# Second mixture of a three-stage kernel: sums of weights between the row tiles, late weight splits moved, 28 filling transposes for 40

## The chip, the cores and the metric

The kernel runs on one core of one Trainium2 chip. The metric is the device time of one execution in microseconds (us). Three runs of the kernel before took 1088.09, 1088.69 and 1091.23 us; their median, 1088.69, is the time before.

## The reference

Three stages follow one another. An attention without softmax makes x from q, k and v; a first mixture of 8 experts sends each of 4608 tokens to its best expert; a second mixture spreads the result over 8 experts of exactly 576 tokens each. The change lies in the second mixture alone:

```python
N, D, E, F = (4608, 512, 8, 1024)
logits = x @ w_gate
# tokens are assigned in order of their logits, at most N // E per expert
for e in range(E):
    mask = assigned == e
    h = np.maximum(x[mask] @ w1[e], 0.0)
    out[mask] = h @ w2[e]
```

## The kernel before

**Precision.** Each f32 operand of a matrix product is held as two parts: a high part, cast on ScalarE (names whi, xqh, and the first half of hx), and a low part, the difference, made on VectorE (wlo, xql, second half of hx). A product is three matmuls: high by high, high by low, low by high.

**The order of the work** is the order in which the program issues it; each of the five engines has its own queue and takes its instructions in that order, waiting where an operand or a buffer is not ready. TensorE (PE) multiplies and transposes, VectorE (DVE) and ScalarE (ACT) prepare operands and empty the accumulators, GpSimd (POOL) issues the gathers of token rows and the scatters of results, and SyncE (SP) issues the loads of weights.

**Expert 0 of the second mixture** is computed plainly. `rows_in(0)` gathers its rows from ybuf (L2064), `warm2` lets TensorE do transposes of a constant while they come (NWARM, L38: 40 of them, L1623). `xplain` (L1649) transposes a tile of 128 rows (tp, two buffers in turn) and splits it (L1654, L1655). `plain1` (L1662) is one of eight product groups of the first layer, 256 weight columns by one half of the tokens, with the relu and its low part (L1659, L1660). The weights are split by `wcast` (L555): the cast on ScalarE (L567), the low part on VectorE (L573), which can be put off into the list CAST; three raw buffers (wraw) rotate, so a load waits for the low part three weights earlier.

**Experts 1 to 7** do the first layer in `seven` (L1907): seven products in place of eight, of sums and differences of weight and input blocks. For these, `first_units` and `rest_units` (generators, one `yield` per step) form the next expert's weights during the work of the one before: sums ws on VectorE (L1793), high parts on ScalarE (L1800), low parts on VectorE (L1797). `xraw` (L1686) transposes a row tile of the next expert and copies it to xb on ScalarE (L1694, L1696); `xsums` forms the sums of inputs (L1708, L1711, L1714).

**The second layer**, `layer2_r` (L2023), has four full row tiles t and a small fifth one. Each full tile is eight groups kf of three matmuls (L2039 to L2041), and after each group `between(t, kf)` issues a piece of the next expert's preparation: a row tile at five places (XAT, L1683) and one step of a generator. The last, small tile is L2035, sixteen matmuls into mD. In the kernel before, the remaining steps of `first_units` run in one go ahead of the second layer (L2112):

```python
run_gen(ga)
gb = rest_units(e + 1)
```

Of the kernel before, what the change touches and what calls it, by code (L numbers as in the profile page):

```python
# [34 lines left out]

PW = (0, 0.8, 2.9, 2.1, 2.0)

NWARM = (18, 40, 6)  # L38

ASIDE = (1, 5, 5, 5, 3)  # L40

# [35 lines left out]
def fused_kernel(ctx, tc, q, k, v, g_norm, emb, tau, w1, w2, wgate, v1, v2, out):  # L77
    nc = tc.nc
    V = nc.vector
# [29 lines left out]
    def mk(pool, shape, dtype, name, **kw):  # L109
        if pool is mp:  # L110
            pool = MP[name in MP0]
        return pool.tile(shape, dtype, name=name, **kw)
# [6 lines left out]
    def src(t, off, ap):  # L119
        return bass.AP(tensor=t.tensor, offset=t.offset + off, ap=ap)  # L120
# [101 lines left out]
    def run_gen(g):  # L222
        for _ in g:
            pass
# [318 lines left out]
    WS = {"load": 0, "cast": 0}  # L543
# [3 lines left out]
    def wload(upto, q=nc.sync):  # L547
        while WS["load"] < min(upto, len(WQ)):
            key, t, off, pat = WQ[WS["load"]]
            raw = mk(wpA, [128, 1024], F32, "wraw", bufs=3)  # L550
            q.dma_start(raw.rearrange("p (a c) -> p a c", c=pat[-1][1]), src(t, off, pat))
            RAW[key] = raw
            WS["load"] += 1

    def wcast(n=1, eng=None, ahead=3, later=None, load=True):  # L555
        for _ in range(n):
            if WS["cast"] >= len(WQ):
                return
            wload(WS["cast"] + 1)
            key = WQ[WS["cast"]][0]  # L560
            raw = RAW.pop(key)

            i = WS["cast"] // (RING // 2)
            wp = WP[(i + (i > 2 * E - 2)) % 2]
            hi = mk(wp, [128, 1024], F32R, "whi")
            lo = mk(wp, [128, 1024], F32R, "wlo")
            nc.scalar.copy(hi, raw)  # L567
            WT[key] = (hi, lo)
            WS["cast"] += 1
            up = WS["cast"] + ahead  # L570

            def rest(eng, lo=lo, raw=raw, hi=hi, up=up):
                eng.tensor_tensor(lo, raw, hi.bitcast(F32), op=OP.subtract)  # L573
                if load:
                    wload(up)
            if later is None:
                rest(eng or V)
            else:
                later.append(rest)
# [292 lines left out]
    def warm(n):  # L872
        pw = mk(psum, [128, 512], F32, "sm")
        for i in range(n):
            nc.tensor.transpose(pw[:, 128 * (i % 4):128 * (i % 4) + 128], ident, ident)
# [45 lines left out]
    for n, st in enumerate(steps):  # L921
        gi, u, hg = st
        i = n % len(UNITS)
# [528 lines left out]
    SIDE, LATER, CAST = [], [], []  # L1452
# [134 lines left out]
    CAST.pop(0)(V)  # L1587
    warm(NWARM[0])
    with tc.If(nc.values_load(fli[0:1, 1:2], min_val=0, max_val=1) > 0, label="gen"):  # L1589
# [30 lines left out]
    def warm2(n):  # L1620
        pw = bank(0)
        for i in range(n):
            nc.tensor.transpose(pw[:, 0, 128 * (i % 4):128 * (i % 4) + 128], ident, ident)  # L1623
# [6 lines left out]
    def turned(e, t, n):  # L1630

        xg = XG.pop((1, e, t))
        pt = mk(ps2, [128, KD, 128], F32, "tp", bufs=2)
        for kd in range(KD):
            nc.tensor.transpose(pt[:, kd, :n], xg[:n, kd * 128:(kd + 1) * 128], ident[:n, :n])  # L1635
        if e == 0 and e not in XQ:
            XQ[e] = [mk(mp, [128, 7, 2, T2], F32R, f"xq{p}") for p in "hl"]
        return xg, pt

    def token(e, t, n, xg):  # L1640

        ti = mk(mp, [128, 1], I32, "ti", bufs=12)
        V.tensor_copy(ti[:n], xg[:n, HD:HD + 1].bitcast(I32))
        TI[e, t] = ti

    def plain_x(e):
        return [x.rearrange("p q k c -> p (q k c)")[:, :KD * C2].rearrange("p (k c) -> p k c", k=KD) for x in XQ[e]]

    def xplain(e, i):  # L1649

        c, t, n = TL[1, e][i]
        xg, pt = turned(e, t, n)
        hi, lo = (x[:, :, 128 * t:128 * t + n] for x in plain_x(e))
        nc.scalar.copy(hi, pt[:, :, :n])  # L1654
        V.tensor_tensor(lo, pt[:, :, :n], hi.bitcast(F32), op=OP.subtract)  # L1655
        token(e, t, n, xg)
# [116 lines left out]
    def sraw(*key):  # L1773
        return SR[SI[key]]

    def sdone(*key):
        over.add(SI[key])
        sload()
# [4 lines left out]
    def unit():  # L1783
        i = UN[0] % 6
        UN[0] += 1
        return [mk(wpB, [128, 1024], F32R, nm) if i < 4 else mk(mp, [128, 1024], F32R, nm, bufs=2) for nm in ("whi", "wlo")]

    def put(e, u, *ng):
        for i, k in enumerate(ng):
            SW[(e, *k)] = [x[:, 512 * i:512 * i + 512].rearrange("p (a c) -> p a c", a=2) for x in u]  # L1790

    def tt(o, a, b, op):
        V.tensor_tensor(o, a, b, op=op)  # L1793

    def lo(u, x, i=None):
        h, l = (u if i is None else [w[:, 512 * i:512 * i + 512] for w in u])
        V.tensor_tensor(l, x, h.bitcast(F32), op=OP.subtract)  # L1797

    def hi(u, x, i=None):
        nc.scalar.copy(u[0] if i is None else u[0][:, 512 * i:512 * i + 512], x)  # L1800
# [26 lines left out]
    def rest_units(e):  # L1827

        sa, sb, a22 = AH[e]
        u2 = unit()  # L1830
        put(e, u2, ("S3", 0), ("S2", 0))
        hi(u2, sa)
        yield
        u3 = unit()
        put(e, u3, ("S1", 0), ("S4", 0))
        hi(u3, sb)
        lo(u2, sa)
        yield
        u4 = unit()
        put(e, u4, ("A22", 0), ("A11", 1))  # L1840
        hi(u4, a22, 0)
        lo(u3, sb)
        yield
        r0, r1 = sraw(e, 0, 1, 0), None
        hi(u4, r0[:, :512], 1)
        lo(u4, a22, 0)
        sdone(e, 0, 0, 1)
        yield
        u5 = unit()
        put(e, u5, ("A12", 1), ("S3", 1))  # L1850
        hi(u5, r0[:, 512:], 0)
        lo(u4, r0[:, :512], 1)
        yield
        r1 = sraw(e, 0, 1, 1)
        a11, a12, a21, a22 = r0[:, :512], r0[:, 512:], r1[:, :512], r1[:, 512:]
        sa, sb = (mk(mp, [128, 1024], F32, "ws", bufs=2) for _ in range(2))
        s2, s1, s3, s4 = sa[:, :512], sa[:, 512:], sb[:, :512], sb[:, 512:]
        tt(s1, a21, a22, OP.add)
        yield
        tt(s2, s1, a11, OP.subtract)  # L1860
        yield
        u6 = unit()
        put(e, u6, ("S2", 1), ("S1", 1))
        hi(u6, sa)
        tt(s3, a11, a21, OP.subtract)
        yield
        hi(u5, s3, 1)
        lo(u5, a12, 0)
        yield
        lo(u6, sa)  # L1870
        yield
        tt(s4, a12, s2, OP.subtract)
        sdone(e, 0, 1, 0)
        yield
        lo(u5, s3, 1)
        AH[e] = s4, a22
        yield
# [191 lines left out]
    rows_in(0)  # L2069
    warm2(NWARM[1])  # L2070
    xplain(0, 0)
    warm2(NWARM[2])
    xplain(0, 1)
    warm2(NWARM[2])
    wload(WS["cast"] + 1, nc.scalar)
    while CAST:
        CAST.pop(0)(V)
    wload(WS["cast"] + 3)
    wcast()
    def step(g, n=1):  # L2080
        for _ in range(n):
            next(g, None)

    def chain(*gs):
        for g in gs:
            yield from g()

    ga = chain(lambda: first_units(1))
    for i, (f, c) in enumerate(((0, 0), (1, 0), (0, 1), (1, 1), (2, 0), (2, 1), (3, 0), (3, 1))):
        plain1(0, f, c, (i + 1) % 3)  # L2090
        if i == 0:
            xplain(0, 2)
            xplain(0, 3)
        if i == 1:
            xplain(0, 4)
        if i < 4:
            wcast()
            if i == 3:
                sload()
        else:  # L2100
            step(ga, 2 if i in (4, 6) else 1)
        if i == 3:
            nc.gpsimd.drain()
            rows_in(1)
    for e in range(E):
        more = e + 1 < E
        if e > 0:
            ga = chain(lambda: first_units(e + 1)) if more else iter(())
            seven(e, ga)
        pairs(e)  # L2110
        if more:
            run_gen(ga)  # L2112
            gb = rest_units(e + 1)
            XS = []

            def between(t, kf):
                if (t, kf) in XAT:
                    xraw(e + 1, XAT[t, kf])
                elif (t, kf) == (1, 5):
                    XS.append(xsums(e + 1))  # L2120
                if XS and kf % 2:
                    step(XS[0])
                else:
                    step(gb)
            layer2_r(e, (0, 1), 0, between)
            layer2_r(e, (2, 3), 1, between)
            run_gen(gb)
            run_gen(XS[0])
            layer2_r(e, (4,), 2)
        else:  # L2130
            for i, tt_ in enumerate(((0, 1), (4,), (2,), (3,))):
                layer2_r(e, tt_, (0, 2, 1, 0)[i])
# [24 lines left out]
```

## Time and profile before

| | |
|---|---|
| median of the runs | 1088.69 us |
| the profiled execution | 1088.42 us, span 1086.6 us |
| TensorE busy | 1026.8 us (94%) |
| VectorE busy | 727.5 us (67%) |
| ScalarE busy | 523.7 us (48%) |
| GpSimd busy | 291.8 us (27%) |
| mean granted TensorE clock | 0.974 of full speed |
| share of the DMA queue of SP | 34.4% |

The span runs from the first to the last instruction of the profiled execution; its own time is 1.8 us longer. Busy is the time in which an engine has an instruction in work. All times in rows are counted from the span's start. The second mixture begins at about 641 us. A wait is idle time of an engine just ahead of an instruction, put down to the instruction that released it.

### The profile page before, as it was taken

How to read it: one execution, taken by the hardware profiler on the slowest of the kernel's cores; microseconds unless marked ns; L12 is line 12 of the kernel's file. 1: busy time of each engine (PE TensorE's matmuls, PEld its weight loads, DVE VectorE, ACT ScalarE, POOL GpSimd, SP SyncE). 2: the span in 40 equal slices, each digit the busy share in tenths (PEclk: the TensorE clock that was granted, in tenths of full speed). 3: DMA queues.
4: the chain of work that ended last, by engine and by line, in shares of the span. 5: the costliest groups of instructions: out<-in, count | busy, mean ns of one | idle time of the engine just before them, and what ended most of it. 6: DMA issues, size and time to landing. Idle time of an engine off the chain costs nothing. (4 is left out here: it accounts for less than half of the span.)

```text
span 1086.6 us, 20563 instructions
## 1 busy us (share of the span) xinstructions
PE 1026.8 (94%) x8237; PEld 942.4 (87%) x8237; DVE 727.5 (67%) x1434; ACT 523.7 (48%) x911; POOL 291.8 (27%) x389
## 2 busy tenths in 40 slices
PE   7888699999999999999999999999999999999998
PEld 7777598999999999999889879897979797979796
DVE  4467965487878696976567656666767676666760
ACT  2567635644536354435441314555555555555551
POOL 2011446516143241616001112221213131212111
PEclk8999799999999999999999999999999999999999
DMA  9999665452524443433311035242424242424211
GB/s 287 380 349 311 211 180 180 143 156 77 186 86 153 121 138 118 134 122 98 117 40 59 26 108 181 87 157 95 149 89 154 87 156 88 157 84 159 80 62 44
DMA packets 94615, 152.35 MB, mean 140 GB/s; under 512 B 11286, under 2 KB 52246, under 8 KB 94514
## 3 DMA queue, kind: packets, MB, share of 16 engines
q1 hardware_dynamic: 84994, 121.65, 34.4%
q0 software_dynamic: 8992, 28.80, 8.3%
q8 instruction: 66, 1.08, 0.4%
q10 hardware_dynamic: 528, 0.52, 0.2%
q14 instruction: 35, 0.29, 0.1%
HBM read 121.14 MB, written 29.82 MB: 139 GB/s over the span
## 5 line engine op out<-in xcount | busy, mean ns | idle before, releaser
L691 PE MATMUL mm<-xh,whi 128*128 128x256 f32 (+8 forms) x512 | 156.0, 305 | 3.4 <-DVE hl L709 3.2
L736 PE MATMUL mm<-hh,whi 128*128 128x256 f32 (+8 forms) x512 | 156.9, 306 | 0.2 <-ACT hh L708 0.2
L692 PE MATMUL mm<-xl,whi 128*128 128x256 f32 (+8 forms) x512 | 153.3, 299 | 0.3 <-DVE xl L662 0.3
L737 PE MATMUL mm<-hl,whi 128*128 128x256 f32 (+8 forms) x512 | 152.4, 298 | 1.1 <-DVE hl L1504 0.6
L693 PE MATMUL mm<-xh,wlo 128*128 128x256 f32 (+8 forms) x512 | 153.2, 299 | 0.0
L738 PE MATMUL mm<-hh,wlo 128*128 128x256 f32 (+8 forms) x512 | 152.1, 297 | 0.0
L833 DVE SCALAR_TENSOR_TENSOR rc<-xg,big 128x512 bf16<-128x512 f32 x128 | 110.9, 867 | 2.6
L573 DVE TENSOR_TENSOR wlo<-wraw,whi 128x1024 fp32r<-128x1024 f32 x72 | 90.7, 1262 | 21.8 <-ACT whi L567 21.3
L691 PEld LDWEIGHTS mm<-xh,whi 128*128 128x128 f32 x512 | 98.3, 192 | 5.0 <-DVE hl L709 3.6
L736 PEld LDWEIGHTS mm<-hh,whi 128*128 128x128 f32 x512 | 97.4, 190 | 2.2 <-ACT hh L708 0.5
L737 PEld LDWEIGHTS mm<-hl,whi 128*128 128x128 f32 x512 | 97.6, 191 | 1.5 <-DVE hl L1504 0.8
L692 PEld LDWEIGHTS mm<-xl,whi 128*128 128x128 f32 x512 | 98.2, 192 | 0.5 <-DVE xl L662 0.5
L693 PEld LDWEIGHTS mm<-xh,wlo 128*128 128x128 f32 x512 | 98.3, 192 | 0.0
L738 PEld LDWEIGHTS mm<-hh,wlo 128*128 128x128 f32 x512 | 97.4, 190 | 0.0
L745 ACT COPY yT<-mm 128x512 f32<-128x512 f32 (+8 forms) x31 | 19.9, 642 | 156.2 <-PE mm L738 156.2
L2054 POOL DMA_INDIRECT out<-tm,ti x40 | 42.5, 1062 | 185.1 <-ACT tm L2052 165.5
L640 POOL DMA_INDIRECT xg<-xbuf,tabi x40 | 43.1, 1077 | 171.5 <-ACT sj L599 77.4
L567 ACT CAST whi<-wraw 128x1024 fp32r<-128x1024 f32 x72 | 75.1, 1046 | 3.7 <-DMA wraw<-in_moe_w 3.7
L708 ACT ACTIVATE hh<-mm 128x512 fp32r<-128x512 f32 (+7 forms) x56 | 36.8, 657 | 73.2 <-PE mm L693 73.2
L1797 DVE TENSOR_TENSOR wlo<-wraw,whi 128x1024 fp32r<-128x1024 f32 (+1 forms) x63 | 60.6, 980 | 11.6 <-ACT whi L1800 11.6
L634 POOL TENSOR_TENSOR xg<-xg,gB 128x512 f32<-128x512 f32 (+7 forms) x37 | 61.7, 1668 | 2.9
L2064 POOL DMA_INDIRECT xg<-ybuf,tab x40 | 44.1, 1103 | 59.1 <-SPq L1589 25.5
(357 smaller groups left out, 2682.4 us busy)
## 6 DMA issues: line engine op xcount, KB each, us to landing
wraw<-in_moe_w SPq DMA_DIRECT2D x127, 512.0 KB, 3.5
kmain<-in_k SPq DMA_DIRECT2D x16, 576.0 KB, 9.0
vmain<-in_v SPq DMA_DIRECT2D x16, 576.0 KB, 10.7
xbuf<-xo SPq DMA_DIRECT2D x16, 528.0 KB, 12.5
ybuf<-yr SPq DMA_DIRECT2D x32, 260.0 KB, 2.2
qmain<-in_q SPq DMA_DIRECT2D x16, 512.0 KB, 9.8
xg<-in_moe_w SPq DMA_DIRECT2D x16, 256.0 KB, 3.9
xg<-in_moe_w_gate SPq DMA_DIRECT2D x8, 256.0 KB, 4.4
```

Source lines behind the costliest of these rows:

```text
L567: nc.scalar.copy(hi, raw)
L573: eng.tensor_tensor(lo, raw, hi.bitcast(F32), op=OP.subtract)
L634: eng.tensor_tensor(x, x, gB[:n, None, :].to_broadcast([n, H, D]), op=OP.mult)
L691: nc.tensor.matmul(o, a, xh[:, kd, :N], start=(kd == 0), stop=False)
L692: nc.tensor.matmul(o, a, xl[:, kd, :N], start=False, stop=False)
L693: nc.tensor.matmul(o, b, xh[:, kd, :N], start=False, stop=(kd == KD - 1))
L736: nc.tensor.matmul(o, a, hh[:, kf, :N], start=(kf == 0), stop=False)
L737: nc.tensor.matmul(o, a, hl[:, kf, :N], start=False, stop=False)
L738: nc.tensor.matmul(o, b, hh[:, kf, :N], start=False, stop=(kf == KF - 1))
L833: V.scalar_tensor_tensor(junk, raws[i], 1.0, wgB[:, x], op0=OP.mult, op1=OP.mult, accum_out=w2g[:, i // KF, i % KF, x:x + 1])
L1797: V.tensor_tensor(l, x, h.bitcast(F32), op=OP.subtract)
L2064: nc.gpsimd.indirect_dma_start(out=xg[:n, :YP], out_offset=None, in_=ybuf[:, :], in_offset=bass.IndirectOffsetOnAxis(ap=tab2[:n, e * SC + ...
```

## The change

Three edits, all in the second mixture:

1. *Filling transposes.* 28 in place of 40 ahead of expert 0's first rows.
2. *Expert 0's late weight splits.* Of the low parts left in CAST, one goes where all went; the next follows the fifth row tile, after the second product group. The five `wcast` that ran ahead of the loop and in its groups 0 to 3 run in groups 1 to 5. Expert 1's raw loads (`sload`) begin in group 5 in place of 3, its `first_units` take one step in group 6 and two in group 7, in place of six steps in groups 4 to 7.
3. *Sums of weights.* The steps of `first_units` that are left after the first layer are no longer run in one go. They are chained ahead of those of `rest_units`, so `between` issues one after each matmul group. Where the chain is used up, the step goes to `xsums`, in even groups too.

```diff
-NWARM = (18, 40, 6)
+NWARM = (18, 28, 6)
...
-    while CAST:
-        CAST.pop(0)(V)
-    wload(WS["cast"] + 3)
-    wcast()
+    CAST.pop(0)(V)
...
         if i == 0:
             xplain(0, 2)
             xplain(0, 3)
+            wload(WS["cast"] + 2)
         if i == 1:
             xplain(0, 4)
-        if i < 4:
+            CAST.pop(0)(V)
+            wload(WS["cast"] + 3)
+        if 0 < i < 6:
             wcast()
-            if i == 3:
+            if i == 5:
                 sload()
-        else:
-            step(ga, 2 if i in (4, 6) else 1)
+        if i > 5:
+            step(ga, i - 5)
...
         if more:
-            run_gen(ga)
-            gb = rest_units(e + 1)
+            gb = chain(lambda: ga, lambda: rest_units(e + 1))
...
-                if XS and kf % 2:
-                    step(XS[0])
-                else:
-                    step(gb)
+                if XS and kf % 2 or next(gb, 0) == 0:
+                    for x in XS:
+                        step(x)
```

ScalarE's queue before, from expert 1's last relu (L1938) into its second layer; whi<-ws is the high part of a unit of sums for expert 2, xb<-tp the copy of a transposed row tile:

```order
L1938 ACTIVATE hx<-tm 128x2x288
L1800 CAST whi<-ws 128x1024
L1694 COPY xb<-tp 128x4x128
L1800 CAST whi<-ws 128x1024
L1800 CAST whi<-wraw 128x512
L1694 COPY xb<-tp 128x4x128
L1800 CAST whi<-wraw 128x512 x2
L1696 COPY xb<-tp 128x8x32
```

The same place of ScalarE's queue in the changed kernel:

```order
L1938 ACTIVATE hx<-tm 128x2x288
L1694 COPY xb<-tp 128x4x128 x2
L1800 CAST whi<-ws 128x1024
L1696 COPY xb<-tp 128x8x32
L1800 CAST whi<-ws 128x1024
L1800 CAST whi<-wraw 128x512 x3
L1694 COPY xb<-tp 128x4x128 x2
```

The copies of row tiles 0 and 1 have moved ahead of the first unit of sums, the small third one ahead of the second unit.

VectorE's queue before, at expert 0's first two product groups; hx<-mB and hx<-mD are the low parts of the hidden layer of groups 0 and 1, xql the low part of a row tile, wlo that of a weight:

```order
L573 TENSOR_TENSOR wlo<-wraw,whi 128x1024 x3
L1660 SCALAR_TENSOR_TENSOR hx<-mB,hx 128x2x256
L1655 TENSOR_TENSOR xql<-tp,xqh 128x4x128
L1643 COPY ti<-xg 128x1
L1655 TENSOR_TENSOR xql<-tp,xqh 128x4x128
L1643 COPY ti<-xg 128x1
L573 TENSOR_TENSOR wlo<-wraw,whi 128x1024
L1660 SCALAR_TENSOR_TENSOR hx<-mD,hx 128x2x256
L1655 TENSOR_TENSOR xql<-tp,xqh 128x4x64
L1643 COPY ti<-xg 64x1
L573 TENSOR_TENSOR wlo<-wraw,whi 128x1024
```

The same place of VectorE's queue in the changed kernel:

```order
L573 TENSOR_TENSOR wlo<-wraw,whi 128x1024
L1660 SCALAR_TENSOR_TENSOR hx<-mB,hx 128x2x256
L1655 TENSOR_TENSOR xql<-tp,xqh 128x4x128
L1643 COPY ti<-xg 128x1
L1655 TENSOR_TENSOR xql<-tp,xqh 128x4x128
L1643 COPY ti<-xg 128x1
L1660 SCALAR_TENSOR_TENSOR hx<-mD,hx 128x2x256
L1655 TENSOR_TENSOR xql<-tp,xqh 128x4x64
L1643 COPY ti<-xg 64x1
L573 TENSOR_TENSOR wlo<-wraw,whi 128x1024 x2
```

Of three splits ahead of the first hidden part one is left, the split ahead of the second one is gone, and two follow the fifth row tile.

## Rows read from the trace of the kernel before

**Rows 1.** The page, part 1: busy us, share of the span, instructions.

```profile
PE 1026.8 (94%) x8237; PEld 942.4 (87%) x8237; DVE 727.5 (67%) x1434; ACT 523.7 (48%) x911; POOL 291.8 (27%) x389
```

**Rows 2.** Waits of TensorE, 700 to 1086 us: total us, times, longest.

```profile
PE tp L1635 <- ACT xb L1694: 14.9, 6, 2.5
```

**Rows 3.** Timeline of TensorE, expert 1: start, duration, instruction, idle before and releaser.

```profile
730.49 0.60 PE L1635 MATMUL tp<-ident,xg 128*128 128x128 f32 x4
...
736.78 0.46 PE L1635 MATMUL tp<-ident,xg 64*128 64x64 f32 x4 [2.47 <-ACT xb L1694]
...
741.86 0.60 PE L1635 MATMUL tp<-ident,xg 128*128 128x128 f32 x4
```

**Rows 4.** Timeline of VectorE, the same place.

```profile
732.86 1.69 DVE L1793 TENSOR_TENSOR ws<-wraw 128x512 f32<-128x512 f32 x2
734.48 0.68 DVE L1793 TENSOR_TENSOR ws<-ws,wraw 128x512 f32<-128x512 f32 x1
```

**Rows 5.** Timeline of ScalarE, the same place.

```profile
730.76 0.69 ACT L1938 ACTIVATE hx<-tm 128x576 fp32r<-128x576 f32 x1 [1.48 <-DVE tm L1932]
735.19 1.04 ACT L1800 CAST whi<-ws 128x1024 fp32r<-128x1024 f32 x1 [3.75 <-DVE ws L1793]
736.14 0.58 ACT L1694 COPY xb<-tp 128x512 f32<-128x512 f32 x1
```

**Rows 6.** Stretches of 2 us: busy time by engine, granted clock, DMA share, GB/s.

```profile
736.00:738.00 2.00, 1.22 (x8) 1.03 (x9) 1.52 (x2) 2.00 (x4) 0.00 (x0) 1.00 0.41 129
...
790.00:792.00 2.00, 2.00 (x9) 1.55 (x9) 1.79 (x4) 2.00 (x4) 0.00 (x0) 0.63 0.82 262
792.00:794.00 2.00, 2.00 (x6) 1.56 (x5) 1.97 (x7) 1.07 (x3) 0.00 (x0) 0.51 0.16 16
```

**Rows 7.** The chain that ended last: the last row tiles of three experts.

```profile
703.32 3.67 PE mD L2035 x16
...
756.41 3.67 PE mD L2035 x16
...
1029.74 3.67 PE mD L2035 x16
```

**Rows 8.** VectorE: timeline at the end of expert 1's layer; waits, 729 to 757 us.

```profile
750.34 2.75 DVE L1711 TENSOR_TENSOR xql<-xb,xqh 128x576 fp32r<-128x576 f32 x4
760.72 0.68 DVE L2050 TENSOR_TENSOR tm<-mD,tm 64x512 f32<-64x512 f32 x1 [7.63 <-ACT tm L2049]
...
DVE wlo L1797 <- ACT whi L1800: 0.5, 2, 0.3
```

**Rows 9.** Timeline of VectorE in expert 0's second layer.

```profile
681.03 1.04 DVE L1793 TENSOR_TENSOR ws<-wraw,ws 128x512 f32<-128x512 f32 x1
...
696.17 2.76 DVE L1711 TENSOR_TENSOR xql<-xb,xqh 128x576 fp32r<-128x576 f32 x4
```

**Rows 10.** Expert 0's product groups: a wait of TensorE; timelines of VectorE and ScalarE.

```profile
PE mA L1672 <- DVE ti L1643: 1.1, 1, 1.1
...
657.80 0.68 DVE L1660 SCALAR_TENSOR_TENSOR hx<-mD,hx 128x512 fp32r<-128x512 f32 x1
658.40 0.41 DVE L1655 TENSOR_TENSOR xql<-tp,xqh 128x256 fp32r<-128x256 f32 x1
...
656.48 0.60 ACT L1659 ACTIVATE hx<-mD 128x512 fp32r<-128x512 f32 x1 [0.49 <-PE mD L1673]
```

**Rows 11.** The fill: timelines of TensorE and GpSimd; landings after issue.

```profile
643.59 3.44 PE L1623 MATMUL mA<-ident 128*128 128x128 f32 x30 [0.92 <-issue]
...
647.95 0.60 PE L1635 MATMUL tp<-ident,xg 128*128 128x128 f32 x4
...
643.41 0.95 POOL L2064 DMA_INDIRECT xg<-ybuf,tab  x1 [0.30 <-issue]
...
xg<-ybuf,tab POOLq DMA_INDIRECT x1, 4.3
...
DMA to landing us min/median/max: 3.2/4.1/6.2
```

## The prediction

> **What bounds the kernel now.** The busy shares come first: TensorE 94% of a span of 1086.6 us, the other engines 67% and less [rows 1]. So the end is set by TensorE, and a change helps only where TensorE stands idle or runs at half clock. The second view is the list of its waits in the seven later experts of the second mixture. There is one kind only: six times, 14.9 us in total, 2.5 us at the longest, the transposes of gathered rows wait for ScalarE's copy xb [rows 2]. The timeline of expert 1 shows one of them: the third tile's transposes start at 736.78 after 2.47 us of idle time [rows 3]. They write a transpose tile (two rotate) whose first user, row tile 0, has not been copied out yet.
>
> Why not is read from the two engines behind it. ScalarE is free at 731.45, but next in its queue stands the high part of a unit made of sums (L1800, whi<-ws). It waits 3.75 us, to 735.19, and the copy of row tile 0 queues behind it and starts at 736.14, although its transposes had ended at 731.09 [rows 3, 5]. That high part waits for the three sums which VectorE makes in one go after the expert's last split, the last one ending at about 735.16 [rows 4].
>
> Each stall costs more than its length. After the one of expert 2 the granted clock is 0.63 and 0.51 in the next two stretches of 2 us, the lower of the two levels, 1.2 GHz; after expert 1's it stays at 1.00 [rows 6]. The chain gives the price: from one expert's last row tile to the next is 53.09 us for expert 1 (703.32 to 756.41), but 54.67 on average for the next five ((1029.74 - 756.41)/5) [rows 7]. The first period holds a stall without a clock drop, so a drop costs 54.67 - 53.09 = 1.58 us.
>
> **The change part by part.** *Sums made one by one.* The four sums (s1, s3, s2, s4) leave the burst and take the first four steps between matmul groups; nothing is added on TensorE. What matters is ScalarE's order: the copies of row tiles 0 and 1 now stand ahead of the first unit of sums. The first can run from 731.45, where ScalarE is free, the second as soon as its own transposes end, so the third tile's transposes find their tile empty at 736.78 - 2.47 = 734.31. The stall goes, six times: **-14.9 us** (bounds 0, if another wait takes its place, and 14.9). With the gaps gone I also take away the five drops: **-7.9 us** (5 x 1.58; bounds 0 and 7.9).
>
> What is late next? VectorE's sums are no earlier than before: s2 still ends near 735.2, the unit's high part runs 735.19 to 736.23 as now, then the copy of the third tile, no longer than the 0.58 us of a full one [rows 5], to about 736.8. The next user of that transpose tile is the fifth set of transposes, at 741.86 now and 739.4 without the stall [rows 3]: 2.6 us of margin. The fourth set uses the other tile, whose copy came second. Further on, the sums of inputs end at 753.1 (750.34 + 2.75) and VectorE then idles 7.63 us [rows 8]; the next products start at 756.41 + 3.67 = 760.08 now and at 757.6 then, so 4.5 us of cover is left for the instructions that were moved. The sums of inputs get more steps late in the layer (once the units are done, odd and even steps serve them), so none is left over for the end. SP's queue of weight loads waits for the same releases by VectorE (s4, the low parts) in the same order, at about the same times.
>
> *Expert 0.* Only three of its six first steps are now done before its second layer, so the low part, s1, s3 and s2 stand ahead of s4, which ended at 682.07. That puts VectorE about 3 us later at the layer's end: 698.93 + 3 = 702, against products at 703.32 + 3.67 = 706.99 [rows 7, 9]. That hides it; without cover it would cost up to 3 us once. Since three loads on SP's queue (two plain tiles and the first raw block for expert 1) wait for low parts made one to two steps later, they go out later too. A cast that waits for one would keep a relu behind it on ScalarE; the second layer reads those values in its third row tile, so I cost this at nothing, within the same 3 us.
>
> *Late weight splits.* On VectorE two splits leave the place ahead of expert 0's first hidden part, and they and later ones go behind the fifth row tile. The hidden layer's second low part now starts at 657.80, behind a split, though its relu on ScalarE is done at 656.48 + 0.60 = 657.08; the fifth tile's low part follows it to 658.81. TensorE waits 1.1 us for that [rows 10]. Without the split both come 0.7 us earlier: **-0.7 us** (bounds 0 and 1.1, the whole wait). The moved splits are due only at the fifth and seventh product group, several us later.
>
> *28 filling transposes.* Thirty take 3.44 us, so twelve take 1.4 us [rows 11]. Whatever that does for the first gathered rows, the second ones, issued at 643.41, landed 4.3 us later, at 647.7, and their transposes start at 647.95 now [rows 11]; 1.4 us earlier would be 646.6. TensorE stands idle for about 1.1 us ahead of them instead, and the gain is **-0.2 us**. Bounds: -1.4, if the rows land earlier, and +1.6, if this gap costs one clock drop at the price above. I take the value nearest to the row that decides, the landing.
>
> The Trainium skill (DMA: Bandwidth & Descriptors, "Anatomy of one DMA — SWDGE (gpsimd) path") gives such a transfer about 2 us plus its bytes at 436 GB/s, for 128 rows of 520 floats an estimate of 2.6 us. By that page the second rows would be there at 646.0 and all of the 1.4 us would be gained, 1063.8 in the end; the 4.3 us of the row speak against it, and the measurement decides.
>
> The sum: 14.9 + 7.9 + 0.7 + 0.2 = 23.7 us off the profiled execution's own 1088.42, 1064.7. The median of the runs shown lies 0.27 above that execution, so **1065.0**.
>
> **The rivals.** *The clock falls all the same.* If the drops come from something other than the gap, only the waits go: 1088.7 - 15.8 = 1072.9. For it: expert 1's gap is as long and cost no clock. Against: the one shown begins right behind its gap [rows 6], and the other four stand at the same place of their periods.
>
> *A new wait at the transposes.* The third tile's copy now stands behind the unit of sums on ScalarE. If ScalarE falls behind there by 1.3 us more than the 2.6 us of margin in each of the six layers, half of the stall returns, too short to cost clock: 1065.0 + 6 x 1.25 = 1072.5. For it: that copy still waits for s2. Against: the margin itself.
>
> *The gathered rows land sooner* in most executions and the shorter fill pays in full: 1063.8. For it: the landings of the gathers there vary between 3.2 and 6.2 us [rows 11]; against: the median of 4.1, which is near the row I used.
>
> *Slower.* The one mechanism large enough is the handover to the next expert: the sums of weights and inputs are spread over more steps, so VectorE and ScalarE might wait for one another at each, and the products of the next expert would wait. It decides from 4.5 us of lengthening on, and to eat 23.7 us in seven handovers it needs 4.5 + 3.4 = 7.9 us in each. Ten us would give 1065.0 + 7 x 5.5 = 1103.5. Against: the instructions are the same ones in another order, and between 736 and 753 VectorE waits for 0.5 us in all now [rows 8].
>
> *The change doesn't do what it says:* if ScalarE's copies still came behind the unit, nothing would move and about 1087.8 would be left. The order of ScalarE's queue speaks plainly against it.
>
> **How the numbers follow.** The forecast 0.78, by itself 1062.5 to 1068; rows landing sooner 0.05; clock falls all the same 0.06; new wait 0.08; slower 0.02; nothing moves 0.01. The range 1062 to 1070 holds the first two, and leaves out 0.17. A difference of 0.3% (3.3 us) is about what a measurement can tell from no change. Faster by more: 0.78 + 0.05 + 0.06 + 0.08 = 0.97; within it 0.01; slower 0.02.
>
> **What would show it.** In the profile after: no wait of the transposes for xb left in TensorE's list; granted clock 1.00 from expert 1 to the end of the layers; 50.6 us (53.09 - 2.47) from one last row tile to the next; on ScalarE two xb copies ahead of the first whi<-ws, which still waits for the sums; expert 0's wait for the low part down from 1.1 to about 0.4 us; a wait of about 1.1 us for the second rows behind the fill. I am wrong if the period stays above 52 us, whatever the wait is then called, or if TensorE waits for weights or inputs at the start of an expert's products.

## The result, and the profile after

| | before | after |
|---|---|---|
| median of the runs | 1088.39 us (1087.05 to 1091.23, 4 runs) | 1063.40 us (1062.60 to 1064.35, 4 runs) |
| span of the profiled execution | 1086.6 us | 1061.9 us |
| mean granted TensorE clock | 0.974 | 0.985 |

The ratio is 0.9767, with a 95% interval of 0.9746 to 0.9789: 25 us faster, where 1065.0 had been forecast from a median that was then 1088.69. The first view is the page's line of busy times, which answers to [rows 1]:

```profile
PE 1015.7 (96%) x8225; PEld 933.9 (88%) x8225; DVE 725.1 (68%) x1434; ACT 525.4 (49%) x911; POOL 294.6 (28%) x389
```

Twelve instructions less on TensorE, the filling transposes; on every other engine the counts are the same. So the change did not save work; it saved waiting and, as the stretches below show, time at the lower clock. Where, is told by the chain of work, which answers to [rows 7]: the last row tiles of experts 0, 1 and 6.

```profile
701.82 3.67 PE mD L2035 x16
752.38 3.67 PE mD L2035 x16
...
1005.02 3.66 PE mD L2035 x16
```

The six periods between the first and the last of these take 303.20 us; before they took 1029.74 - 703.32 = 326.42. That is 23.22 of the 24.7 us between the two spans. The rest can be placed too. From the first filling transpose to expert 0's last row tile it is 61.07 us (640.75 to 701.82) against 61.93 (641.39 to 703.32), 0.86 less. The fill itself began 0.64 sooner, through stages ahead of it that were not changed: chance. From 1005.02 to the end it is 56.9 us, as before (1086.6 - 1029.74).

The list of TensorE's waits from 640 us to the end (total, times, longest), which answers to [rows 2, 10], has six entries of one wait each, and none of them lies behind 660 us. The five longest:

```profile
PE mA L1623 <- issue: 0.9, 1, 0.9
PE tp L1635 <- DMA xg<-ybuf,tab: 0.7, 1, 0.7
PE mA L1671 <- ACT xqh L1654: 0.6, 1, 0.6
PE mA L1623 <- PEq L1589: 0.4, 1, 0.4
PE mA L1672 <- DVE xql L1655: 0.4, 1, 0.4
```

ScalarE's timeline at the place of [rows 5] shows why:

```profile
729.27 0.69 ACT L1938 ACTIVATE hx<-tm 128x576 fp32r<-128x576 f32 x1 [1.48 <-DVE tm L1932]
729.86 0.57 ACT L1694 COPY xb<-tp 128x512 f32<-128x512 f32 x1
731.46 0.59 ACT L1694 COPY xb<-tp 128x512 f32<-128x512 f32 x1 [1.03 <-PE tp L1635]
733.71 1.05 ACT L1800 CAST whi<-ws 128x1024 fp32r<-128x1024 f32 x1 [1.66 <-DVE ws L1793]
734.66 0.36 ACT L1696 COPY xb<-tp 128x256 f32<-128x256 f32 x1
```

The first copy runs right behind the last relu, the second as soon as its own transposes end. The unit of sums still waits for VectorE, but the one copy behind it, the third, ends at 735.02, ahead of the transposes that use its tile next (737.83, below). TensorE's third and fifth sets of transposes, against [rows 3]:

```profile
732.75 0.46 PE L1635 MATMUL tp<-ident,xg 64*128 64x64 f32 x4
...
737.83 0.60 PE L1635 MATMUL tp<-ident,xg 128*128 128x128 f32 x4
```

No wait stands at either. And the two stretches of 2 us in which the clock was low behind expert 2's stall [rows 6] have the full clock (the seventh figure, ahead of the DMA share), as has every other one from 640 us to TensorE's last product:

```profile
790.00:792.00 2.00, 2.00 (x10) 1.67 (x9) 2.00 (x5) 1.26 (x2) 0.00 (x0) 1.00 0.62 217
792.00:794.00 2.00, 2.00 (x10) 1.59 (x10) 2.00 (x3) 2.00 (x5) 0.00 (x0) 1.00 0.00 0
```

### The profile page after: what moved, and what is told of

Its sections match the earlier page's. It is cut to its first block, busy times and chain, and to the rows that moved or that the text cites. A ratio compares the mean times of both kernels' runs of the same rounds, so it can differ in the third digit from the quotient of the medians.

```text
span 1061.9 us, 20538 instructions
## 1 busy us (share of the span) xinstructions
PE 1015.7 (96%) x8225; PEld 933.9 (88%) x8225; DVE 725.1 (68%) x1434; ACT 525.4 (49%) x911; POOL 294.6 (28%) x389
```

## The experiments

Each median stands beside a median of the kernel before from the same chip: 1091.0 us for the runs with the third edit alone, with the other two alone, with the order alone and with 40 transposes; 1089.3 for all gaps filled and for the two runs with additions whose scratch tile is zeroed first; 1092.7 for the run that zeroes it late and the two with some gaps filled. A ratio is a run's time over that of the kernel before, with its 95% interval.

**The third edit alone.** The kernel before with

```diff
-            run_gen(ga)
-            gb = rest_units(e + 1)
+            gb = chain(lambda: ga, lambda: rest_units(e + 1))
...
-                if XS and kf % 2:
-                    step(XS[0])
-                else:
-                    step(gb)
+                if XS and kf % 2 or next(gb, 0) == 0:
+                    for x in XS:
+                        step(x)
```

> The kernel before with the third edit alone (sums of weights between the row tiles). My theory: it carries the six waits and the five clock drops, 14.9 + 7.9 = 22.8 us, so about 1065.6 us, with no wait of the transposes for xb left and 50.6 us from one last row tile to the next. Rival: the edits in expert 0 carry a good part of the gain (by more than 0.9 us): then above 1068 us.

Measured: 1066.2 us, ratio 0.9773 (0.9736 to 0.9811). The chain's first and last row tile of the six periods:

```profile
705.94 3.67 PE mD L2035 x16
...
1009.14 3.66 PE mD L2035 x16
```

303.20 us, the same as with all three edits. The third edit carries the whole gain of the periods. What this execution lost, it lost in expert 0, and there is something to learn from it. Three waits stand close together at the fifth row tile's transposes and first products, in TensorE's timeline; the last line below is VectorE's:

```profile
657.28 0.46 PE L1635 MATMUL tp<-ident,xg 64*128 64x64 f32 x4 [0.49 <-DVE ti L1643]
...
658.20 0.41 PE L1671 MATMUL mA<-xqh,whi 128*128 128x320 f32 x1 [0.46 <-ACT xqh L1654]
660.06 0.41 PE L1672 MATMUL mA<-xql,whi 128*128 128x320 f32 x1 [1.45 <-DVE ti L1643]
...
654.80 1.23 DVE L573 TENSOR_TENSOR wlo<-wraw,whi 128x1024 fp32r<-128x1024 f32 x1 [2.33 <-ACT whi L567]
```

The weight split ahead of the first hidden part waited 2.33 us for ScalarE's cast, against 1.38 us in the profile of the kernel before, and what TensorE waits for stands behind it on VectorE. The waits are longer, and the clock falls behind them, which it did not in the profiled execution of the kernel before:

```profile
660.00:662.00 2.00, 1.94 (x10) 1.95 (x11) 1.19 (x3) 0.00 (x0) 1.81 (x1) 0.76 0.83 218
662.00:664.00 2.00, 2.00 (x10) 2.00 (x9) 0.00 (x0) 0.00 (x0) 0.91 (x2) 0.50 0.89 316
```

From the first filling transpose to expert 0's last row tile it took 64.15 us (641.79 to 705.94), 2.2 more than before. In the changed kernel that split comes behind the fifth row tile. So the second edit may also remove a chance of a clock drop, which I had not counted; one execution suggests it and does not show it, since of the other four profiles with the splits unmoved none has this drop.

**The other two edits alone.** The changed kernel with

```diff
-            gb = chain(lambda: ga, lambda: rest_units(e + 1))
+            run_gen(ga)
+            gb = rest_units(e + 1)
```

and the old lines in `between`.

> The changed kernel with the third edit undone (sums in one go ahead of the second layer), the moved splits and the 28 transposes kept. My theory: the six waits and the clock drops of experts 1 to 6 come back, and a seventh wait of about 2.6 us comes up in expert 0, whose burst now holds the low part and three sums ahead of the unit of sums: 1088.4 - 0.9 + 2.6 = 1090.1 us, 1091.7 with one more clock drop. Rival: expert 0's moved steps cost nothing by themselves: 1087.5 us, six waits.

Measured: 1092.2 us, ratio 1.003 (1.0007 to 1.0053); seven waits, the first of them in expert 0:

```profile
PE tp L1635 <- ACT xb L1694: 17.6, 7, 2.7
...
684.55 0.46 PE L1635 MATMUL tp<-ident,xg 64*128 64x64 f32 x4 [2.70 <-ACT xb L1694]
```

The theory's 2.6 us against 2.70. The clock stayed up behind this new first gap and fell behind each of the other six, the "one more drop". The second edit without the third is a small loss, here together with the first: fewer early steps are done, and the burst that is left needs the third edit.

**Only the order, the sums still in one go.** The changed kernel with

```diff
-            gb = chain(lambda: ga, lambda: rest_units(e + 1))
+            run_gen(ga)
+            gb = chain(lambda: iter([None] * 4), lambda: rest_units(e + 1))
```

> The changed kernel with the four sums in one go again, but the first unit of sums (its high part on ScalarE) still held back by four steps. My theory: only ScalarE's order counts, two copies of row tiles ahead of the unit; so as the changed kernel, 1063.4 +- 1 us, and no wait for xb. Rival: the sums must be spread between the groups of matmuls: waits of VectorE or ScalarE come back, 1070 us or more.

Measured: 1062.6 us, ratio 0.9753 (0.9715 to 0.9791), which is the changed kernel's within the intervals. TensorE has no wait behind 660 us. VectorE and ScalarE:

```profile
729.84 1.70 DVE L1793 TENSOR_TENSOR ws<-wraw 128x512 f32<-128x512 f32 x2
731.46 0.68 DVE L1793 TENSOR_TENSOR ws<-ws,wraw 128x512 f32<-128x512 f32 x1
732.17 0.69 DVE L1793 TENSOR_TENSOR ws<-wraw,ws 128x512 f32<-128x512 f32 x1
...
728.33 0.57 ACT L1694 COPY xb<-tp 128x512 f32<-128x512 f32 x1
729.92 0.59 ACT L1694 COPY xb<-tp 128x512 f32<-128x512 f32 x1 [1.02 <-PE tp L1635]
732.17 1.05 ACT L1800 CAST whi<-ws 128x1024 fp32r<-128x1024 f32 x1 [1.66 <-DVE ws L1793]
```

The four sums run back to back on VectorE, as in [rows 4]. What made the kernel faster is that the unit of sums comes four steps later in ScalarE's queue, behind two copies; that the sums are made one by one is beside the point. (The third edit's last lines, which give steps to `xsums` in even groups too, are in this run as well; no run takes them out alone.)

**The gaps filled.** The kernel before with

```diff
             def between(t, kf):
+                if (t, kf) == (0, 5) and e > 0:
+                    pw = bank(2)
+                    for _ in range(10):
+                        nc.tensor.matmul(pw[:, 0, :], HX[e][:, 0, 0, 0, :128], wb(1, e, 0)[0], start=True, stop=True)
```

> The kernel before, with ten extra matmuls of 128x512 (2.3 us, results unused) into the idle third accumulator ahead of the third tile's transposes in experts 1 to 6, so that TensorE works while it waits. My theory: idle gaps cause the clock drops, so the waits for xb shrink to about 0.1 us in the list while the time that they take stays, and the clock stays at 1.00: 1088.4 - 7.9 = 1080.5 us, 53.1 us from one last row tile to the next in all six. Rival: the drops have another cause and stay: 1088.4 us, 54.7 us in five of six.

Measured: 1081.4 us, ratio 0.9916 (0.9888 to 0.9944). The extra matmuls stand where the gap was, and the chain's ends of the six periods are

```profile
735.04 2.46 PE L2120 MATMUL mD<-whi,hx 128*128 128x512 f32 x10
...
704.22 3.67 PE mD L2035 x16
...
1022.80 3.66 PE mD L2035 x16
```

53.10 us each on average (318.58/6), with a clock of 1.00 throughout. Nothing was made earlier here; keeping TensorE at work took 7.8 us out of the same six periods (326.42 - 318.58). This is the share of the clock, and 318.58 - 303.20 = 15.4 us is that of the waits: the gaps cause the drops.

**40 transposes in the changed kernel.** One number: `NWARM = (18, 40, 6)`.

> The changed kernel with 40 filling transposes in place of 28. My theory: from the first filling transpose to the first matmul with a low part of rows 8.56 us as before in place of 8.37, so 0.2 us more, 1063.6, not to be told from 1063.4 by time; no wait for the second gathered rows. Rival: the fill is on the path in full, 1.4 us more, 1064.8 us.

Measured: 1063.1 us, ratio 0.9764 (0.9720 to 0.9808). TensorE's timeline at the two ends of the measure:

```profile
637.61 1.28 PE L1623 MATMUL mA<-ident 128*128 128x128 f32 x10 [0.45 <-PEq L1589]
...
646.11 0.39 PE L1672 MATMUL mB<-xql,whi 128*128 128x256 f32 x1 [0.20 <-DVE ti L1643]
```

8.50 us, against 8.37 with 28 and 8.56 before; and no wait for the second rows. The first edit is worth 0.1 to 0.2 us, which no time shows.

**More work on VectorE.** The changed kernel with a scratch tile dz, zeroed on GpSimd, and

```diff
             def between(t, kf):
+                if t == 0:
+                    V.tensor_tensor(dz, dz, dz, op=OP.add)
```

> The changed kernel with eight extra additions of 128x512 on VectorE (0.6 us each, 4.8 us) in each second layer of experts 0 to 6, one after each group of the first row tile. My theory: 4.5 us of cover at the next expert's products, 2.6 us at the fifth transposes (three additions come ahead of the sum that matters there, 1.8 us): nothing shows, 1063.4 +- 1 us. Rival: VectorE's chain is close to the path already: 4.8 us in each of seven layers, up to 1097 us.

Measured: 1067.8 us, ratio 0.9796 (0.9765 to 0.9828), by its time a miss for my theory. But the six periods are untouched: 706.27 to 1009.48, 303.21 us, and no wait stands in them. The 4 us lie in expert 0: from the first filling transpose to its last row tile it takes 64.82 us (641.45 to 706.27) against 61.07. The first rows came late behind my own zeroing of the scratch tile, but that delayed the first product with a low part by 0.7 us only (9.11 us behind the first filling transpose, against 8.37). The larger part is a wait for ScalarE's cast of the fifth row tile, 2.48 us against 0.56 in the changed kernel, with a low clock behind it:

```profile
642.10 0.53 POOL L2070 MEMSET dz<- 128x512 f32 x1 [25.47 <-SPq L1589]
642.81 1.03 POOL L2064 DMA_INDIRECT xg<-ybuf,tab  x1 [0.19 <-issue]
...
647.41 0.66 PE L1635 MATMUL tp<-ident,xg 128*128 128x128 f32 x4 [2.04 <-DMA xg<-ybuf,tab]
...
659.94 0.42 PE L1671 MATMUL mA<-xqh,whi 128*128 128x320 f32 x1 [2.48 <-ACT xqh L1654]
...
660.00:662.00 2.00, 1.96 (x7) 1.73 (x8) 2.00 (x4) 0.83 (x1) 0.87 (x1) 0.64 0.23 85
```

What held ScalarE there is not shown.

The same run with the zeroing behind the gathers:

> The run with eight extra additions again, the scratch tile now zeroed on GpSimd behind the gathers of expert 0's rows instead of ahead of them. My theory: the 4 us that the first of these runs lost lay all in expert 0's first rows, which came late behind that zeroing; so 1063.4 +- 1 us now. Rival: the additions cost them: 1067.8 us again.

Measured: 1063.2 us, ratio 0.9723 (0.9691 to 0.9755); 303.21 us for the six periods again. The eight additions cost nothing. The 4 us went with the place of the zeroing, but not simply by the late rows: the next run zeroes first too, its first rows are as late (1.77 us), and its wait for that cast is 0.56 us.

**Twice as much.** `if t < 2`, sixteen additions, with the zeroing where it was at first.

> The same with sixteen extra additions (9.6 us), after each group of the first two row tiles. By the 4.5 us of cover that I predicted with, products wait 5.1 us in each of seven handovers: 1063.4 + 36 = 1099 us. Rival: the last low parts are needed only by the third product and later (3.2 us and more behind the first), so the true cover is near 9 us and little shows: below 1070 us.

Measured: 1081.4 us, ratio 0.9925 (0.9903 to 0.9946). Neither number was right. TensorE has one new wait, once in each handover, and the timelines show where:

```profile
PE mB L1923 <- ACT tm L2052: 12.3, 7, 2.0
...
755.90 0.67 ACT L1708 CAST xqh<-xb 128x576 fp32r<-128x576 f32 x1 [2.90 <-DVE xb L1714]
...
760.67 1.07 ACT L2052 COPY tm<-mB 128x512 f32<-128x512 f32 x2
...
761.79 0.40 PE L1923 MATMUL mB<-xqh,whi 128*128 128x288 f32 x1 [1.70 <-ACT tm L2052]
```

It is no operand of the products that is late. The second product needs accumulator mB, and the copies that empty it stand on ScalarE behind the casts of the sums of inputs, which wait for VectorE. With 9.6 us more on VectorE that is 1.7 us late, so the cover of the handover is near 8 us; 4.5 us, from the end of VectorE's sums to the first product, was too small, and the place was another. One of these seven waits, of 1.74 us at 814.38, has a clock of 0.74 and 0.50 in the two stretches from 814 us; behind the other six the clock stayed up.

**Which gaps cost the clock.** The filled gaps again, on the kernel before, in expert 1 alone (`e == 1`), and in experts 2, 4 and 6 (`e in (2, 4, 6)`).

> The kernel before with the ten extra matmuls in expert 1's gap alone. Theory A: the first gap after a long busy stretch leaves the clock up, whichever expert it is in; then expert 2's gap is free of a drop now and experts 3 to 6 have one each: 53.1, 53.1, 54.7, 54.7, 54.7, 54.7 us from one last row tile to the next, 1086.8 us. Theory B: the point in time decides, expert 1's gap only falls well: 53.1 and then five times 54.7 us, 1088.4 us.

> The kernel before with the extra matmuls in the gaps of experts 2, 4 and 6. Theory A (the first gap is free, each later one costs a drop): 53.1 us for experts 1, 2, 4 and 6, 54.7 for 3 and 5, 1088.4 - 3 x 1.58 = 1083.7 us. Theory B (the point in time decides): any of the gaps of 3 and 5 may be free too, down to 1080.5 us.

One run each, 1092.6 and 1080.9 us. (In the first the second mixture began 4.5 us later than in the profile of the kernel before, so the periods are compared, not the times.) With expert 1's gap filled the chain reads

```profile
707.57 3.67 PE mD L2035 x16
760.67 3.67 PE mD L2035 x16
815.35 3.67 PE mD L2035 x16
```

53.10, then 54.68 us: expert 2's gap, now the first, cost its drop, and so did the four behind it. Theory A is wrong. In the other run two of the three gaps left (experts 1 and 3) cost none, and expert 5's did, though they are of one length. The third of the four rows below to the fourth is expert 5's period, 54.68 us; expert 3's, from the first to the second, is 53.08:

```profile
808.25 3.68 PE mD L2035 x16
861.33 3.67 PE mD L2035 x16
914.43 3.67 PE mD L2035 x16
969.11 3.67 PE mD L2035 x16
```

and the two gaps in TensorE's timeline:

```profile
841.71 0.46 PE L1635 MATMUL tp<-ident,xg 64*128 64x64 f32 x4 [2.47 <-ACT xb L1694]
...
947.87 0.46 PE L1635 MATMUL tp<-ident,xg 64*128 64x64 f32 x4 [2.50 <-ACT xb L1694]
```

So a gap of 2.5 us may or may not cost the clock, and neither its order nor the expert decides. The moment at which it falls may decide, as theory B has it, or what TensorE did before it; these runs do not show which.

## Why the prediction was right

**The stall and its cause: right.** The wait of the transposes went in all six experts, and the run with the order alone shows that ScalarE's queue was the cause, as the prediction read it from three timelines. Its term was 14.9 us; measured it is 15.4, because behind a gap the transposes can no longer overlap with the matmuls ahead of them, which the wait does not count: in the profile after the third set starts at 732.75, 0.07 us before the matmul ahead of it ends (732.42 + 0.40), and 0.07 or 0.08 us before it in the other five experts.

**The clock: right.** 7.9 us forecast, 7.8 measured by the filled gaps. The price of a drop, 1.58 us, had been read as the difference of two periods, one with and one without; the six periods of 53.06 to 53.12 us with the gaps filled confirm the one without. That there were five drops to remove had been counted in one execution; where every second gap was filled two of three gaps cost none, so the number may differ from one execution to the next, and its fit is in part luck. The rival "the clock falls all the same" (1072.9) is out by the run with all gaps filled.

**What comes next: right in its result.** The third copy ended at 735.02, ahead of transposes at 737.83: 2.8 us of margin against 2.6. The sums of inputs ended at 751.04, ahead of products at 752.38 + 3.67 = 756.05: 5.0 us against 4.5. In expert 0 VectorE ended at 700.79 (forecast 702, against a stage that began 0.64 us later). The rivals "new wait" and "slower" lived on these margins, and the second has more room than I gave it: it begins at about 8 us of lengthening, through accumulator mB, not at 4.5 through the operands.

**Expert 0: right, by 0.86 us against 0.9.** The split's share is the wait for the low part, 1.06 us less 0.38, the forecast 0.7. In the profile after VectorE has the hidden part right behind its relu, against [rows 10]:

```profile
656.30 0.69 DVE L1660 SCALAR_TENSOR_TENSOR hx<-mD,hx 128x512 fp32r<-128x512 f32 x1 [1.60 <-ACT hx L1659]
```

**The fill: right, 0.2 us.** The second rows were issued at 642.82, and their transposes start at 647.07 behind a wait of 0.74 us (1.1 forecast), 4.25 us later:

```profile
645.01 0.66 PE L1635 MATMUL tp<-ident,xg 128*128 128x128 f32 x4
...
647.07 0.66 PE L1635 MATMUL tp<-ident,xg 128*128 128x128 f32 x4 [0.74 <-DMA xg<-ybuf,tab]
```

By the estimate of 2.6 us from the Trainium skill (DMA: Bandwidth & Descriptors, "Anatomy of one DMA — SWDGE (gpsimd) path") they would have landed at 645.4, ahead of the 646.33 at which TensorE was free, and there would have been no wait; the trace disagrees, in this execution too.

**What was missed** is small: the overlap of the transposes (0.5 us), and that the splits left in their old place may cost a clock drop in expert 0, as in one execution. The forecast of 1065.0 rested on a median 0.3 us above the one measured beside the result, and 0.64 us of the profile's gain came from stages that were not changed.

## What to carry to other kernels

Where the engine that sets the time waits for a buffer, look at the queue of the engine that empties it: a short copy behind an instruction that waits for somebody else has to wait with it. Here 3.75 us of ScalarE's waiting became 2.47 us of TensorE's, and moving the waiting instruction back behind two copies cured it, with no operation saved. Price a gap of TensorE by the period that it stands in, with and without a clock drop, not by its length alone: here 15.4 us of gaps cost 23.2. And compare kernels stage by stage: the stages ahead of this change began the second mixture anywhere from 637.6 to 645.9 us in these profiles, while the sum of the six periods behind it agreed to 0.01 us in the six profiles with the third edit and no wait in them.

## What had not been expected

The clock at a gap: five of the six gaps of about 2.5 us cost a drop of 1.57 us in the kernel before, six of seven in the run without the third edit, all five that were left where expert 1's was filled, but only one of three where every second gap was filled. Shorter ones can cost it too: one of seven of 1.7 to 2.0 us did in the run with sixteen additions. And a cluster of three waits of 0.5, 0.5 and 1.4 us, with work between them, cost a drop as well.
